# w2 at the turn between two decode layers, in six column blocks instead of four

## The chip, the cores and the metric

The kernel runs on one core of a Trainium2 chip. The metric is device time in microseconds (us) from start to end of one execution; lower is better. A time of this kernel before is the median of three executions. The core's engines are TensorE (PE, its weight loads PEld), VectorE (DVE), ScalarE (ACT), GpSimd (POOL) and SyncE (SP), which here does nothing but issue DMAs. The DMAs of SP are spread over 16 DMA engines.

## The reference

One decode step of 8 sequences goes through two identical layers (the same weights and caches serve both). A layer is attention over a cache of 4096 positions, with 32 query heads on 4 key/value heads of 128, and then a dense block with a gelu:

```
x = x + _A_ref(_layernorm(x), k_cache, v_cache, wq, wo)   # q = x @ wq; softmax(q k) v; @ wo
x = x + _B_ref(_layernorm(x), w1, b1, w2, b2)             # gelu(x @ w1 + b1) @ w2 + b2
(and both lines once more)
```

Everything is fp32. Sizes: x (8, 1, 1024); k_cache and v_cache (8, 4, 4096, 128); wq (1024, 4096); wo (4096, 1024); w1 (1024, 3584); w2 (3584, 1024).

## The kernel before

All data lies in one tile `arena` of 52 units; a unit is 1024 columns by 128 partitions (0.52 MB). `stream` is a list, written out by hand, of every DMA in its order, each with the unit at which it must land. `pump()` walks this list: it issues a DMA as soon as the units of its place are free, and stops at the first that are not. `release(slot)` frees units when the PE work that reads them has been emitted, and pumps again. So SP issues in the order of the list, and each issue waits for the last matmul that read the place.

Layer 0 reads wq, all K and V of batches 0 to 7, wo, w1 and w2; layer 1 goes through the batches from 7 down to 0, and reads K and V, wo and w1 again. wq stays in the arena from layer 0 to layer 1 (units 0 to 27 and some parked pieces), so it is read once; w2 stays from the turn to the end of layer 1.

The place of the change is the turn, the function `swap()`. There the dense block of layer 0 computes its second product, h @ w2, one column block after another, and each finished block gives two tiles of 128 rows of the new x. With each such tile kt, the query product of layer 1 can be advanced by that tile's rows of wq: `used(kt, u)` does half u (4 matmuls of 512 columns, in two accumulators) and releases the wq units, into which parts of w2 and then K tiles of layer 1 are loaded. The layernorm's mean and scale are applied afterwards (`moments`).

For a column block, `down` adds 28 row tiles (kt 0 to 27; the last four are `LAST`) in four groups of 32 partitions, DVE copies the result out (L512), two small matmuls with `bsel` sum the four groups and turn them (L516), and DVE adds them to x (L518); then come the `used` calls (L361). In the trace every fp32 matmul is two records.

In layer 1 the product with w2 is made by `down_row`, from the w2 parts that are still held; the rows `LAST` of the first 512 columns are released at the turn and read again at the end (`LATE`).

Of the kernel before, what the change touches and what calls it, by code (L numbers as in the profile page):

```python
# [10 lines left out]
ALU = mybir.AluOpType  # L11
# [3 lines left out]
P = 128  # L15
B, D = 8, 1024
# [3 lines left out]
NT = D // P  # L20
# [13 lines left out]
SCW = W // 2  # L34
N_UNIT = 52
OWN = N_UNIT - 1
UNPARK = 14
XS = B + 1
CB = D // Q4
LAST = NFT - 4  # L40
W2_PARTS = (((0, 16, 40), (16, 8, 44), (LAST, 4, 46)), ((0, 4, 47), (4, 16, 48), (20, 4, 46), (LAST, 4, 0)),
            ((LAST, 4, 1), (0, 16, 2), (16, 8, 6)), ((LAST, 4, 0), (0, 16, 8), (16, 8, 12)))
LATE_AT = 14
LATE_C = 2
LATE = ((0, 2), (2, 1), (3, 1))
# [60 lines left out]
def decode_layers(ctx: ExitStack, tc: tile.TileContext, x, kc, vc, wq, wo, w1, w2, out):  # L106
# [352 lines left out]

    w2_at = {}  # L460

    def down(y, c, kts, n0=0):

        for n, kt in enumerate(kts, n0):
            g = kt % 4
            nc.tensor.matmul(y[32 * g:32 * g + 32], h_at(kt), w2_at[c, kt], start=(n < 4), stop=(n >= NFT - 4))  # L466

    def down_row(y, kts, cs=range(CB)):

        for kt in kts:  # L470
            for c in cs:
                nc.tensor.matmul(y[32 * c:32 * c + 32], h_at(kt), w2_at[c, kt], start=(kt == 0), stop=(kt == NFT - 1))  # L472

    def w2_kts(c, i):

        k0, n, _ = W2_PARTS[c][i]
        return range(k0, k0 + n)

    def arrive(key, kts):
        slot = held[key]  # L480
        for e, kt in enumerate(kts):
            w2_at[key[1], kt] = slot.ap[:, e * Q4:(e + 1) * Q4]
        return kts

    def swap():

        ys = small_ps("s")
        nc.vector.tensor_tensor(xv, xv, b2T.unsqueeze(2).to_broadcast([P, NT, B]), ALU.add)
        pt = small_ps("pt")
        late = []  # L490
        acc = q_acc()
        stats = ()

        def used(kt, u):
            slot = held.pop(("q", kt, u))
            q_part(acc, u, kt, 0, slot.ap)
            release(slot)
            if (kt, u) == (4, 0):
                st["unparked"] = unpark()

        for c in range(CB):
            y = ys[:, c % 2 * Q4:(c % 2 + 1) * Q4]
            n = 0
            for i in range(len(W2_PARTS[c])):
                kts = arrive(("w2", c, i), w2_kts(c, i))
                down(y, c, kts, n)
                n += len(kts)
            slot = held.pop(("w2", c, [k0 for k0, _, _ in W2_PARTS[c]].index(LAST)))
            if c < LATE_C:
                release(slot)  # L510
            ysb = row_s[:, c % 2 * Q4:(c % 2 + 1) * Q4]
            nc.vector.tensor_copy(ysb, y)  # L512
            while late:
                late.pop()()
            for i in range(2):
                nc.tensor.matmul(pt[:, i * B:(i + 1) * B], ysb[:, i * P:(i + 1) * P], bsel, start=True, stop=True)  # L516
            xc = xv[:, 2 * c:2 * c + 2]
            nc.vector.tensor_tensor(xc, pt[:, 0:2 * B].rearrange("p (i b) -> p i b", b=B), xc, ALU.add)  # L518
            if c == CB - 1:
                stats = moments(pt)  # L520
            for kt in (2 * c, 2 * c + 1):
                for u in range(2):
                    if kt < NT - 1:
                        late.append(lambda kt=kt, u=u: used(kt, u))
                        if (kt, u) != (3, 1):
                            late.pop()()
                    elif u == 0:
                        spot = st.pop("unparked")
                        q_part(acc, u, kt, 0, spot.ap)
                        spot.free()  # L530
                    else:
                        slot = held.pop(("qe", 0))
                        q_part(acc, u, kt, 0, slot.ap)
                        q_part(acc, u, kt, W - KEEP, spare)
                        slot.free()
                    if c == CB - 1 and (kt, u) in ((NT - 2, 1), (NT - 1, 0)):
                        next(stats, None)
# [217 lines left out]
    def fixed(*at):  # L755
        return lambda k, i: (at[i],)

    def down_weights(key, c, kts, at):
        k0, k1 = c * NFT + kts[0], c * NFT + kts[-1] + 1
        stream.append((key, (k1 - k0) // 4, w2[0][:, k0 * Q4:k1 * Q4], (at,), ()))  # L760

    def listed(*spots):
        spots = iter(spots)
# [17 lines left out]
    for c in range(CB):  # L781
        for i, (_, _, at) in enumerate(W2_PARTS[c]):
            down_weights(("w2", c, i), c, w2_kts(c, i), at)
    stream.append((("qe", 0), 0, wq[0][:, -W:-KEEP], x_row[:, 0:W - KEEP], ()))
    batch(1, last_b, ((4, 16), (4, 20), (4, 24), (2, 14), (2, 16)), ((4, 20),))
    batch(1, last_b - 1, ((4, 24), (4, 16), (2, 14), (4, 20), (2, 36)), ((8, 28), (8, 16)))
    batch(1, last_b - 2, ((4, 36), (4, 24), (8, 28)), ((8, 16), (8, 24)))
    at = [32, 16, 24] * (4 * B)
    for b in orders[1][3:]:
# [10 lines left out]
    for layer in range(2):  # L800
        st["layer"] = layer
        b2_row = spare[:, SCW:SCW + Q4]
        hooks = {("probs", last_b): opened} if layer == 0 else {
            ("v", *v_at(last_b - 2, 0)): lambda: bias_row(b2_row, spare[:, SCW + Q4:SCW + Q4 + CH]),
            ("v", *v_at(last_b - 1, 1)): rebuild,
            ("v", *v_at(last_b - 3, 0)): bias_diag}
        last = attention(orders[layer], kept if layer == 0 else (), hooks)
        rsum = row_sums()
        project(f"o{layer}", oT, x_row, rsum, {4: last})
        rs = layernorm(x_row, rsum)  # L810
        if layer == 0:
            idle(CH)
            expand("i0", rs)
            idle(CH, Q4)
            swap()
        else:
            nc.vector.tensor_tensor(x_row, x_row, b2_row, ALU.add)
            y = []

            def turn_next():  # L820
                pending.pop(0)()

            def grow(kts, cs=range(CB)):
                if not y:
                    y.append(small_ps("s")[:, 0:Q4])
                down_row(y[0], kts, cs)

            def grown(u):
                return lambda: grow(range(GT * u, GT * (u + 1)))

            work = {u: [grown(u - 1), turn_next] for u in range(1, WIDE)}
            work[0] = [turn_next]
            work[1].append(scaled_x)
            work[WIDE] = [grown(WIDE - 1)]
            for e, kt in enumerate((3, 5)):
# [87 lines left out]
```

## Time and profile before

| | |
|---|---|
| median of 3 executions | 848.56 us (848.41 to 848.66) |
| profiled execution, its own time | 848.87 us |
| its span, first to last instruction | 847.0 us |
| busy: PE, DVE, ACT | 535.8, 192.4, 55.4 us |
| DMA | 358.51 MB, mean 423 GB/s |
| mean granted TensorE clock | 0.821 of full speed |

The span is what lies between the first and the last instruction; the execution's own time is 1.87 us longer. Busy time is a mean over stages with different limits, so it doesn't tell which engine sets the end. In the chain of waits, a row "DMA arena<-in_k_dram" starts with the issue of that DMA and lasts until its data has landed, so start plus length is the landing.

### The profile page before, as it was taken

What the parts mean: (1) busy time and instruction counts of PE and PEld (TensorE: products, weight loads), DVE (VectorE), ACT (ScalarE), POOL (GpSimd) and SP (SyncE); (2) the same over time, 40 slices, a digit from 0 to 9 for tenths busy, and PEclk for the clock granted to TensorE, in tenths of its full rate; (3) what the DMA queues carried; (4) which work ended last, traced back from release to release, by engine and by line L of the source; (5) the groups of instructions that cost most, each with busy time, mean ns of one, the idle gap of its engine ahead of it and who ended that gap; (6) DMA issues with size and microseconds to landing.
All of it is one profiled execution on the core that took longest, in us unless ns stands there. A gap on an engine that the chain in (4) does not pass through costs nothing.

```text
span 847.0 us, 9470 instructions
## 1 busy us (share of the span) xinstructions
PE 535.8 (63%) x4120; PEld 179.1 (21%) x4120; DVE 192.4 (23%) x636; ACT 55.4 (7%) x118; POOL 2.4 (0%) x14
## 2 busy tenths in 40 slices
PE   0755565656656657677778775476666576655677
PEld 0221111111111111133243222111111121212334
DVE  0013132313222231300010242232414132222011
ACT  0110000000000000000201100000000000000021
POOL 0000000000000000000000000000000000000000
PEclk9977779676876877699999897968768768788899
DMA  9999999999999999999999999999999999999997
GB/s 402 420 423 430 433 433 431 426 436 427 424 428 435 434 432 421 427 429 424 429 409 413 399 427 438 429 430 435 425 438 426 434 429 433 431 426 434 421 426 285
DMA packets 19768, 358.51 MB, mean 423 GB/s; under 512 B 2192, under 2 KB 2576, under 8 KB 4112
## 3 DMA queue, kind: packets, MB, share of 16 engines
q1 hardware_dynamic: 19584, 357.77, 99.2%
q8 instruction: 32, 0.52, 0.3%
q10 hardware_dynamic: 144, 0.15, 0.1%
q14 instruction: 8, 0.07, 0.0%
HBM read 357.78 MB, written 0.13 MB: 423 GB/s over the span
## 4 chain that ended last, share of the span: by engine, by line
DMA 73%; PE 23%; DVE 2%; issue 1%; another core or an unknown queue 1%; ACT 0%; SPq 0%; ACTq 0%; DVEq 0%
DMA arena<-in_k_dram 28%; DMA arena<-in_v_dram 21%; DMA arena<-in_w_dram 10%; DMA arena<-in_wo_dram 8%; PE sps L595 8%; PE o_ps L638 7%; DMA arena<-in_wq_dram 5%; PE y L424 2%; PE acc L361 1%; PE sps L472 1%; PE acc L306 1%; PE sps L650 1%; PE acc L303 0%; PE sps L346 0%
## 5 line engine op out<-in xcount | busy, mean ns | idle before, releaser
L595 PE MATMUL sps<-arena,qz 128*32 128x512 f32 x1024 | 162.3, 777 | 118.9 <-DMA arena<-in_k_dram 117.0
L638 PE MATMUL o_ps<-arena 128*32 128x512 f32 x512 | 87.4, 816 | 48.2 <-DMA arena<-in_v_dram 36.7
L638 PE MATMUL o_ps<-arena,spare 128*32 128x512 f32 x512 | 84.9, 782 | 40.9 <-DMA arena<-in_v_dram 34.0
L595 PEld LDWEIGHTS sps<-arena,qz 128*32 128x32 f32 x1024 | 37.7, 132 | 208.2 <-issue 169.8
L643 DVE SCALAR_TENSOR_TENSOR scr<-o_ps,bits,scr 128x128 f32<-128x128 f32 x192 | 67.3, 351 | 6.8
L641 DVE TENSOR_SCALAR scr<-o_ps,bits 128x128 f32<-128x128 f32 x64 | 22.4, 351 | 144.6 <-PE o_ps L638 144.6
L424 PE MATMUL y<-arena,oxT 128*32 128x256 f32 x512 | 37.8, 441 | 23.5 <-DMA arena<-in_wo_dram 23.5
L361 PE MATMUL acc<-arena,oxT 128*32 128x512 f32 x248 | 32.9, 671 | 6.3 <-DMA arena<-in_wq_dram 4.9
L650 PEld LDWEIGHTS sps<-bits,scr 128*128 128x128 f32 x128 | 21.7, 213 | 67.6 <-issue 48.3
L638 PEld LDWEIGHTS o_ps<-arena 128*32 128x32 f32 x512 | 16.9, 134 | 81.4 <-issue 49.1
L638 PEld LDWEIGHTS o_ps<-arena,spare 128*32 128x32 f32 x512 | 17.2, 131 | 71.7 <-issue 47.1
L600 DVE TENSOR_SCALAR_CACHE_REDUCE arena<-sps 128x512 f32<-128x512 f32 x16 | 11.1, 691 | 91.4 <-PE sps L595 91.4
L651 DVE TENSOR_TENSOR oxT<-sps,scr 128x8 f32<-128x8 f32 x64 | 10.5, 164 | 87.1 <-PE sps L650 87.1
L600 DVE TENSOR_SCALAR_CACHE_REDUCE spare<-sps 128x512 f32<-128x512 f32 x16 | 11.1, 691 | 82.4 <-PE sps L595 82.4
L619 ACT ACTIVATE sps<-arena,bits 128x512 f32<-128x512 f32 x16 | 10.9, 681 | 285.2 <-DVE scr L613 285.2
L619 ACT ACTIVATE sps<-spare,bits 128x512 f32<-128x512 f32 x16 | 10.9, 681 | 263.6 <-DVE scr L613 263.6
L650 PE MATMUL sps<-bits,scr 128*128 128x8 f32 x128 | 27.6, 288 | 0.0
L424 PEld LDWEIGHTS y<-arena,oxT 128*32 128x32 f32 x512 | 18.0, 125 | 44.0 <-DMA arena<-in_wo_dram 25.9
L303 PE MATMUL acc<-arena,oxT 128*32 128x512 f32 x160 | 20.7, 631 | 9.2 <-DMA arena<-in_w_dram 9.2
L184 PE MATMUL sps<-spare,ident 128*32 128x512 f32 (+2 forms) x60 | 24.9, 533 | 0.6 <-DVE scr L217 0.6
L609 PE MATMUL sps<-scr,bits 128*128 128x128 f32 x32 | 7.6, 322 | 22.9 <-DVE scr L605 22.9
L466 PE MATMUL sps<-arena,oxT 128*32 128x256 f32 x224 | 14.2, 382 | 5.6 <-DMA arena<-in_w_dram 5.6
(134 smaller groups left out, 248.8 us busy)
## 6 DMA issues: line engine op xcount, KB each, us to landing
arena<-in_v_dram SPq DMA_DIRECT2D x25, 4096.0 KB, 21.6
arena<-in_k_dram SPq DMA_DIRECT2D x21, 4096.0 KB, 20.6
arena<-in_k_dram SPq DMA_DIRECT2D x20, 2048.0 KB, 18.2
arena<-in_w_dram SPq DMA_DIRECT2D x16, 2048.0 KB, 12.7
arena<-in_v_dram SPq DMA_DIRECT2D x11, 2048.0 KB, 19.7
arena<-in_wo_dram SPq DMA_DIRECT2D x8, 2048.0 KB, 13.0
arena<-in_wo_dram SPq DMA_DIRECT2D x3, 4096.0 KB, 24.2
arena<-in_w_dram SPq DMA_DIRECT2D x6, 1024.0 KB, 19.6
```

The source lines that it names most:

```text
L184: nc.tensor.matmul(ps[0:32, 0:w], ident[:, 0:32], spare[:, 0:w], start=True, stop=True)
L303: nc.tensor.matmul(acc[32 * j:32 * j + 32, :], lhs, slot.ap[:, c:c + CH], start=(kt < 4), stop=(kt >= NT - 4))
L361: nc.tensor.matmul(acc[u][32 * j:32 * j + 32, d0 - j * CH:d1 - j * CH], xnT[:, kt * XS:kt * XS + 32], ap[:, d0 - c0:d1 - c0], start=(kt == ...
L424: nc.tensor.matmul(y[32 * j:32 * j + 32, 0:Q4], lhs[:, n * B:n * B + 32], slot.ap[:, c + j * Q4:c + (j + 1) * Q4], start=(n == 0), stop=(n ...
L466: nc.tensor.matmul(y[32 * g:32 * g + 32], h_at(kt), w2_at[c, kt], start=(n < 4), stop=(n >= NFT - 4))
L595: nc.tensor.matmul(ps[32 * g:32 * g + 32, :], qz[:, c:c + 32], kt[:, g * CH:(g + 1) * CH], start=(j == 0), stop=(j == HKV - 1))
L600: nc.vector.tensor_scalar(st["row", b].ap[:, half * CH:(half + 1) * CH], ps, SCALE, None, op0=ALU.mult, op1=ALU.max, accum_out=st["mx", b] ...
L619: nc.scalar.activation(pp, row[:, h * CH:(h + 1) * CH], AF.Exp, bias=bias, scale=1.0, accum_out=ls[:, h:h + 1])
L638: nc.tensor.matmul(o[32 * g:32 * g + 32, :], s[:, g], v[:, g * CH:(g + 1) * CH], start=(half == 0), stop=(half == NH - 1))
L641: nc.vector.tensor_scalar(r, o[:, 0:P], sel_t[:, 0:1], None, op0=ALU.mult)
L643: nc.vector.scalar_tensor_tensor(r, o[:, t * P:(t + 1) * P], sel_t[:, t:t + 1], r, op0=ALU.mult, op1=ALU.add)
L650: nc.tensor.matmul(po[:, 0:REP], r_s[j % 2], sel_h, start=True, stop=True)
```

## The change

w2 is cut at the turn into blocks of 128, 128, 256, 256, 128 and 128 columns (`BLOCKS`) instead of four of 256. `W2_STREAM` gives each part as first column tile, column tiles, first row tile, row tiles, unit. The last four rows of the last two blocks come in one DMA. `Q_TURN` says which halves of wq tiles are used ahead of the turning matmuls and which behind the addition of each block. The K tiles of layer 1's first two batches get other places and another order, and the unparked wq piece goes to unit 16 instead of 14.

```diff
-UNPARK = 14
+UNPARK = 16
-W2_PARTS = (((0, 16, 40), (16, 8, 44), (LAST, 4, 46)), ((0, 4, 47), (4, 16, 48), (20, 4, 46), (LAST, 4, 0)),
-            ((LAST, 4, 1), (0, 16, 2), (16, 8, 6)), ((LAST, 4, 0), (0, 16, 8), (16, 8, 12)))
+BLOCKS = ((0, 1), (1, 1), (2, 2), (4, 2), (6, 1), (7, 1))
+W2_STREAM = ((0, 1, 0, 24, 40), (0, 1, LAST, 4, 43), (1, 1, 0, 24, 44), (1, 1, LAST, 4, 47),
+             (2, 2, 0, 16, 48), (2, 2, LAST, 4, 43), (4, 2, LAST, 4, 47), (2, 2, 16, 8, 0),
+             (4, 2, 0, 16, 2), (4, 2, 16, 8, 6),
+             (6, 2, LAST, 4, 43), (6, 1, 0, 16, 8), (6, 1, 16, 8, 12), (7, 1, 0, 16, 10), (7, 1, 16, 8, 13))
+Q_TURN = (((), ((0, 0), (0, 1))), ((), ((1, 0), (1, 1))), ((), ((2, 0), (3, 0), (2, 1))),
+          (((3, 1),), ((4, 0), (4, 1), (5, 0))), (((5, 1),), ((6, 0),)), ((), ((6, 1),)))
...
-        for c in range(CB):
-            y = ys[:, c % 2 * Q4:(c % 2 + 1) * Q4]
+        for c, (k0, nk) in enumerate(BLOCKS):
+            w = nk * P
+            y = ys[:, c % 2 * Q4:c % 2 * Q4 + w]
...
-            while late:
-                late.pop()()
-            for i in range(2):
+            for kt, u in Q_TURN[c][0]:
+                used(kt, u)
+            for i in range(nk):
                 nc.tensor.matmul(pt[:, i * B:(i + 1) * B], ysb[:, i * P:(i + 1) * P], bsel, start=True, stop=True)
...
+            for kt, u in Q_TURN[c][1]:
+                used(kt, u)
+        next(stats, None)
+        spot = st.pop("unparked")
...
-    batch(1, last_b, ((4, 16), (4, 20), (4, 24), (2, 14), (2, 16)), ((4, 20),))
-    batch(1, last_b - 1, ((4, 24), (4, 16), (2, 14), (4, 20), (2, 36)), ((8, 28), (8, 16)))
+    batch(1, last_b, ((2, 14), (2, 18), (4, 20), (4, 24), (2, 16), (2, 14)), ((4, 20),))
+    batch(1, last_b - 1, ((2, 18), (4, 24), (4, 14), (4, 20), (2, 36)), ((8, 28), (8, 16)))
```

In `batch`, a pair is (units, first unit).

**On PE, from the first block of w2 to the last use of wq.** L466 is `down`, L516 the turning matmuls, L361 the query product. Before:

```order
L466 MATMUL sps<-arena,oxT 32x256 x28
L516 MATMUL sps<-bits,scr 128x8 x2
L361 MATMUL acc<-arena,oxT 32x512 x12
L466 MATMUL sps<-arena,oxT 32x256 x28
L361 MATMUL acc<-arena,oxT 32x512 x4
L516 MATMUL sps<-bits,scr 128x8 x2
L361 MATMUL acc<-arena,oxT 32x512 x16
L466 MATMUL sps<-arena,oxT 32x256 x28
L516 MATMUL sps<-bits,scr 128x8 x2
L361 MATMUL acc<-arena,oxT 32x512 x8
L564 MATMUL sps<-oxT,bits 128x8
```

The same place now, from the third block's end on (L481 is `down`, L527 the turning matmuls, L368 the query product):

```order
L368 MATMUL acc<-arena,oxT 32x512 x12
L481 MATMUL sps<-arena,oxT 32x256 x28
L368 MATMUL acc<-arena,oxT 32x512 x4
L527 MATMUL sps<-bits,scr 128x8 x2
L368 MATMUL acc<-arena,oxT 32x512 x12
L481 MATMUL sps<-arena,oxT 32x128 x28
L368 MATMUL acc<-arena,oxT 32x512 x4
L527 MATMUL sps<-bits,scr 128x8
L368 MATMUL acc<-arena,oxT 32x512 x4
L481 MATMUL sps<-arena,oxT 32x128 x28
L527 MATMUL sps<-bits,scr 128x8
L368 MATMUL acc<-arena,oxT 32x512 x4
```

Behind the last block there is now one half of a wq tile (x4) where there were two (x8), and the last two blocks have half the columns.

**On SP, from the last w2 parts to the third batch piece of layer 1.** Before:

```order
L268 DMA arena<-in_w_dram 128x4096
L268 DMA arena<-in_w_dram 128x2048
L268 DMA xb<-in_wq_dram 128x128
L268 DMA arena<-in_k_dram 128x4096 x3
L268 DMA arena<-in_k_dram 128x2048 x2
L268 DMA arena<-in_v_dram 128x4096
```

Now:

```order
L275 DMA arena<-in_w_dram 128x2048
L275 DMA arena<-in_w_dram 128x1024
L275 DMA arena<-in_w_dram 128x2048
L275 DMA arena<-in_w_dram 128x1024
L275 DMA xb<-in_wq_dram 128x128
L275 DMA arena<-in_k_dram 128x2048 x2
L275 DMA arena<-in_k_dram 128x4096 x2
L275 DMA arena<-in_k_dram 128x2048 x2
L275 DMA arena<-in_v_dram 128x4096
```

The last 6144 columns of w2 before wq's piece come in four DMAs instead of two, and the first K batch of layer 1 in six instead of five. Over the whole program SP issues 139 DMAs instead of 136, of the same bytes.

## Rows read from the trace of the kernel before

**Rows 1.** The page: busy share of the DMA engines in 40 slices.

```profile
DMA  9999999999999999999999999999999999999997
```

**Rows 2.** Windows ahead of the turn and over it: PE, PEld, DVE, ACT, POOL, PEclk, DMA, GB/s.

```profile
395.00:430.00 35.00, 26.23 (x245) 10.47 (x244) 3.47 (x15) 7.78 (x15) 0.00 (x0) 1.00 1.01 428
...
440.00:490.00 50.00, 39.99 (x396) 15.56 (x392) 9.22 (x34) 5.40 (x6) 0.20 (x1) 0.93 1.00 403
```

**Rows 3.** Chain of waits, DMAs at the turn and later: start us, us, what.

```profile
413.08 12.66 DMA arena<-in_w_dram
...
442.60 5.41 DMA arena<-in_w_dram
...
452.96 13.67 DMA arena<-in_w_dram
...
480.99 5.88 DMA arena<-in_k_dram
...
501.93 19.93 DMA arena<-in_v_dram
...
653.15 24.85 DMA arena<-in_v_dram
...
684.76 22.37 DMA arena<-in_k_dram
```

**Rows 4.** Chain of waits, work of PE and DVE at the turn.

```profile
448.06 0.68 PE sps L466 x8
...
450.12 2.83 PE acc L361 x24
...
466.68 1.11 PE sps L466 x16
...
476.79 0.70 DVE spare L542
...
479.87 1.10 PE sps L595 x8
```

**Rows 5.** Timeline of SP at the turn, single DMA issues: start us, us, what.

```profile
440.14 0.33 SPq L268 DMA_DIRECT2D arena<-in_w_dram  x1
...
463.20 0.33 SPq L268 DMA_DIRECT2D arena<-in_k_dram  x1
...
473.28 0.33 SPq L268 DMA_DIRECT2D arena<-in_k_dram  x1
...
475.54 0.33 SPq L268 DMA_DIRECT2D arena<-in_k_dram  x1
...
483.56 0.33 SPq L268 DMA_DIRECT2D arena<-in_v_dram  x1
```

**Rows 6.** DMA view, KB and us to landing: those issued at 440.14, 463.20, 475.54.

```profile
arena<-in_w_dram SPq DMA_DIRECT2D x1, 512.0 KB, 6.6
...
arena<-in_k_dram SPq DMA_DIRECT2D x1, 2048.0 KB, 13.4
...
arena<-in_k_dram SPq DMA_DIRECT2D x1, 1024.0 KB, 8.8
```

**Rows 7.** PE's groups by shape from 425 to 470 us: 256 and 128 columns.

```profile
L466 PE MATMUL sps<-arena,oxT 128*32 128x256 f32 x224 | 14.2, 382 | 5.6 <-DMA arena<-in_w_dram 5.6
...
L306 PE MATMUL acc<-arena,oxT 128*32 128x128 f32 x128 | 3.9, 274 | 2.2 <-DMA arena<-in_w_dram 2.2
```

**Rows 8.** Windows of 5 us in which the clock falls, columns as in rows 2.

```profile
465.00:470.00 5.00, 2.81 (x32) 1.55 (x28) 0.87 (x3) 0.00 (x0) 0.00 (x0) 0.83 1.02 436
470.00:475.00 5.00, 5.00 (x26) 1.10 (x18) 0.88 (x4) 0.00 (x0) 0.00 (x0) 0.50 0.99 390
```

**Rows 9.** DMA view, whole run: a DMA on an empty queue; instruction fetches.

```profile
out_dram<-xb SPq DMA_DIRECT2D x1, 128.0 KB, 1.7
...
q8 instruction: 32, 0.52, 0.3%
```

More of the change, by code (lines that the diff above doesn't have):

```diff
@@ L40 @@
 LAST = NFT - 4
-W2_PARTS = (((0, 16, 40), (16, 8, 44), (LAST, 4, 46)), ((0, 4, 47), (4, 16, 48), (20, 4, 46), (LAST, 4, 0)),
-            ((LAST, 4, 1), (0, 16, 2), (16, 8, 6)), ((LAST, 4, 0), (0, 16, 8), (16, 8, 12)))
+BLOCKS = ((0, 1), (1, 1), (2, 2), (4, 2), (6, 1), (7, 1))
[3 more added lines that the diff above has]
+             (6, 2, LAST, 4, 43), (6, 1, 0, 16, 8), (6, 1, 16, 8, 12), (7, 1, 0, 16, 10), (7, 1, 16, 8, 13))
+W2_OF = (((0, 0, 24), (0, LAST, 4)), ((1, 0, 24), (1, LAST, 4)), ((2, 0, 16), (2, LAST, 4), (2, 16, 8)),
+         ((4, LAST, 4), (4, 0, 16), (4, 16, 8)), ((6, LAST, 4), (6, 0, 16), (6, 16, 8)), ((6, LAST, 4), (7, 0, 16), (7, 16, 8)))
+Q_TURN = (((), ((0, 0), (0, 1))), ((), ((1, 0), (1, 1))), ((), ((2, 0), (3, 0), (2, 1))),
+          (((3, 1),), ((4, 0), (4, 1), (5, 0))), (((5, 1),), ((6, 0),)), ((), ((6, 1),)))
 LATE_AT = 14
@@ L460, in decode_layers, with w2_ap @@
     w2_at = {}
+    def w2_ap(k0, nk, kt):
+        at = [w2_at[k0 + i, kt] for i in range(nk)]
+        ap = at[0]
+        if nk == 2:
+            ap = bass.AP(ap.tensor, ap.offset, [ap.ap[0], (at[1].offset - ap.offset, 2), (1, P)])
+        return ap
     def down(y, c, kts, n0=0):
@@ L465, in down @@
             g = kt % 4
-            nc.tensor.matmul(y[32 * g:32 * g + 32], h_at(kt), w2_at[c, kt], start=(n < 4), stop=(n >= NFT - 4))
+            nc.tensor.matmul(y[32 * g:32 * g + 32], h_at(kt), w2_ap(*BLOCKS[c], kt), start=(n < 4), stop=(n >= NFT - 4))
     def down_row(y, kts, cs=range(CB)):
@@ L471, in down_row, with arrive @@
             for c in cs:
[L472 to L483, printed above, removed]
+                nc.tensor.matmul(y[32 * c:32 * c + 32], h_at(kt), w2_ap(2 * c, 2, kt), start=(kt == 0), stop=(kt == NFT - 1))
+    def arrive(key):
+        k0, nk, kt0, n = key[1:]
+        for e in range(n):
+            for i in range(nk):
+                at = (e * nk + i) * P
+                w2_at[k0 + i, kt0 + e] = held[key].ap[:, at:at + P]
     def swap():
@@ L489, in swap @@
         pt = small_ps("pt")
-        late = []
         acc = q_acc()
-        stats = ()
         def used(kt, u):
@@ L499, in used @@
                 st["unparked"] = unpark()
-        for c in range(CB):
-            y = ys[:, c % 2 * Q4:(c % 2 + 1) * Q4]
+        for c, (k0, nk) in enumerate(BLOCKS):
+            w = nk * P
+            y = ys[:, c % 2 * Q4:c % 2 * Q4 + w]
             n = 0
[L504 to L511, printed above, removed]
+            for of, kt0, nkt in W2_OF[c]:
+                key = next(("w2", *part[:4]) for part in W2_STREAM if (part[0], part[2]) == (of, kt0))
+                arrive(key)
+                down(y, c, range(kt0, kt0 + nkt), n)
+                n += nkt
+                if kt0 == LAST and k0 < LATE_C * 2:
+                    release(held.pop(key))
+            ysb = row_s[:, c % 2 * Q4:c % 2 * Q4 + w]
@@ L512, in swap @@
             nc.vector.tensor_copy(ysb, y)
-            while late:
-                late.pop()()
-            for i in range(2):
+            for kt, u in Q_TURN[c][0]:
+                used(kt, u)
+            for i in range(nk):
                 nc.tensor.matmul(pt[:, i * B:(i + 1) * B], ysb[:, i * P:(i + 1) * P], bsel, start=True, stop=True)
-            xc = xv[:, 2 * c:2 * c + 2]
-            nc.vector.tensor_tensor(xc, pt[:, 0:2 * B].rearrange("p (i b) -> p i b", b=B), xc, ALU.add)
-            if c == CB - 1:
+            xc = xv[:, k0:k0 + nk]
@@ L520, in swap @@
+            nc.vector.tensor_tensor(xc, pt[:, 0:nk * B].rearrange("p (i b) -> p i b", b=B), xc, ALU.add)
+            if c == len(BLOCKS) - 1:
                 stats = moments(pt)
[L521 to L537, printed above, removed]
+            for kt, u in Q_TURN[c][1]:
+                used(kt, u)
@@ L538, in swap @@
+        next(stats, None)
+        spot = st.pop("unparked")
+        q_part(acc, 0, NT - 1, 0, spot.ap)
+        spot.free()
+        next(stats, None)
+        slot = held.pop(("qe", 0))
+        q_part(acc, 1, NT - 1, 0, slot.ap)
+        q_part(acc, 1, NT - 1, W - KEEP, spare)
+        slot.free()
         arena.own_ap = spare[:, 0:SCW]
@@ L756, in fixed, with down_weights @@
         return lambda k, i: (at[i],)
-    def down_weights(key, c, kts, at):
-        k0, k1 = c * NFT + kts[0], c * NFT + kts[-1] + 1
-        stream.append((key, (k1 - k0) // 4, w2[0][:, k0 * Q4:k1 * Q4], (at,), ()))
+    def down_weights():
+        c0 = 0
+        for *part, at in W2_STREAM:
+            cols = part[1] * part[3] * P
+            stream.append((("w2", *part), -(-cols // SCW), w2[0][:, c0:c0 + cols], (at,), ()))
+            c0 += cols
     def listed(*spots):
@@ L780, in decode_layers @@
     weights(("i0",), w1[0], [4] * 7, fixed(48, 40, 44, 48, 40, 44, 48))
-    for c in range(CB):
-        for i, (_, _, at) in enumerate(W2_PARTS[c]):
-            down_weights(("w2", c, i), c, w2_kts(c, i), at)
+    down_weights()
     stream.append((("qe", 0), 0, wq[0][:, -W:-KEEP], x_row[:, 0:W - KEEP], ()))
-    batch(1, last_b, ((4, 16), (4, 20), (4, 24), (2, 14), (2, 16)), ((4, 20),))
-    batch(1, last_b - 1, ((4, 24), (4, 16), (2, 14), (4, 20), (2, 36)), ((8, 28), (8, 16)))
+    batch(1, last_b, ((2, 14), (2, 18), (4, 20), (4, 24), (2, 16), (2, 14)), ((4, 20),))
+    batch(1, last_b - 1, ((2, 18), (4, 24), (4, 14), (4, 20), (2, 36)), ((8, 28), (8, 16)))
     batch(1, last_b - 2, ((4, 36), (4, 24), (8, 28)), ((8, 16), (8, 24)))
@@ L841, in decode_layers @@
                 for i in range(n):
-                    for c in range(LATE_C):
-                        at = (i * LATE_C + c) * Q4
-                        w2_at[c, LAST + e + i] = ap[:, at:at + Q4]
+                    for k in range(2 * LATE_C):
+                        at = (i * 2 * LATE_C + k) * P
+                        w2_at[k, LAST + e + i] = ap[:, at:at + P]
                 grow(range(LAST + e, LAST + e + n))
@@ L881, in _blocks @@
     import numpy as _np
-    a = w.reshape(NFT, P, CB, Q4).transpose(1, 2, 0, 3)
-    late = a[:, 0:LATE_C, LAST:].transpose(0, 2, 1, 3)
-    return _np.concatenate([a.reshape(P, -1), late.reshape(P, -1)], 1)[None]
+    a = w.reshape(NFT, P, D).transpose(1, 0, 2)
+    parts = [a[:, t:t + n, k * P:(k + nk) * P] for k, nk, t, n, _ in W2_STREAM] + [a[:, LAST:, 0:LATE_C * Q4]]
+    return _np.concatenate([part.reshape(P, -1) for part in parts], 1)[None]
 def _start(x, b1, b2):
```

## The prediction

> **What bounds the kernel.** I began with the slices of the DMA engines: their busy share reads 9 from the first slice to the last but one [rows 1]. So the time is that of one stream of transfers, and an edit is worth what it takes out of that stream or adds to it. Then I asked where the stream runs below its pace. Ahead of the turn it moves 428 GB/s; over the 50 us of the turn 403, at a busy share of 1.00 all the same [rows 2]. Had the turn run at 428, it would have taken 50 x 403 / 428 = 47.1 us: 2.9 us is all that can be won there.
>
> Next, what part of this 2.9 us comes from SP issuing late, since that alone is what other places and another order can mend. A DMA's landing is set by the slowest of the 16 engines, so I go by landings. The price of a transfer: one of 2048 KB (2.097 MB) takes 4.90 us at 428 GB/s [rows 2]; one of 4096 KB takes 9.71, since landings at 678.00 and 707.13 stand three such DMAs apart [rows 3]. Two halves cost 2 x 4.90 - 9.71 = 0.09 us more than the whole, so that a DMA costs about 0.08 us fixed, and 1024 KB takes 2.49, 512 KB 1.28, 1536 KB 3.69, 256 KB 0.68 (estimates from these two). The chain's landings then give a balance, stretch by stretch [rows 3]:
> - 425.74 to 448.01: two DMAs of 2048 KB and one of 1024, two of 512, one of 2048, two of 512, worth 22.3 us; it took 22.27. Nothing lost.
> - 448.01 to 466.63: 512, 2048, 1024, 512, 2048 and 1024 KB, worth 17.3; it took 18.62. Lost 1.3.
> - 466.63 to 486.87: wq's 64 KB (0.2), three of 2048, two of 1024, worth 19.9; it took 20.24. Lost 0.4.
> - 486.87 to 521.86: four of 2048, two of 1024, one of 4096, worth 34.3; it took 34.99. Lost 0.7.
>
> Against this I hold the lead of an issue: how long before the landing of the previous DMA it comes. The DMA issued at 463.20 landed 13.4 us later, at 476.6, and its successor was issued at 473.28: a lead of 3.3. The next one was issued at 475.54 and landed at 484.3, and the one behind it came at 480.99: 3.3 again. That one landed at 486.87, and V's issue at 483.56 had 3.3 as well [rows 3, 5, 6]. These three leads lie on the stretch that lost 0.4. On the first stretch the DMA issued at 440.14 landed at 446.7, and its successor came at 442.60, a lead of 4.1 [rows 3, 5, 6]: that stretch lost nothing. So a lead of 4.1 is long enough for the slowest engine, and one of 3.3 costs 0.1 to 0.2. The 1.3 and the 0.7 have no short lead that I can put them to: the DMA that landed at 466.63 had been issued 13.67 earlier [rows 3]. They may be engines held up by instruction fetches, of which there are 32 in the run [rows 9]; the change doesn't take those away.
>
> **The change, part by part.**
>
> *Three more DMAs.* Two more for w2, one more for K, the bytes the same: 3 x 0.09 = 0.27 us on a queue that is never empty. The bounds: zero, if the short pieces hide behind the slower engines, and 3 x 1.7 = 5.1, if each cost what a DMA on an empty queue takes to land [rows 9]. I take 0.27: the 2048 KB DMAs of the trace stand in a full queue just as these will. Here a rule speaks against the change. The Trainium skill (DMA: Bandwidth & Descriptors, "Anatomy of one DMA — SWDGE (gpsimd) path") fits a DMA's time as about 2.0 us fixed plus its bytes, for DMAs issued by GpSimd; three more would be 6 us by it. In this trace that fixed part overlaps the transfer of the DMA ahead.
>
> *More pieces on PE and DVE.* `down` has 168 matmuls instead of 112, but the same columns: a 256-column block is 56 records at 14.2 / 224 = 0.063 us, 3.4 us; a 128-column block 56 at 3.9 / 128 = 0.030, 1.7 us [rows 7]. Four of the one cost what two of the one and four of the other cost, 13.6 us. Each block also pays the way from its last matmul over copy, turning matmuls and addition to the next: 448.74 to 450.12, 1.4 us [rows 4]. There are two more, 2.8 us of PE idle at most; the DMA queue covers them as long as the leads hold, which the next part works out. The 112 more records and their weight loads are about one more instruction fetch: zero to 1.3 us (the largest loss above), I take 0.
>
> *Other places and another order.* Here is the timetable of the changed turn. Landings follow from 425.74 and the prices: w1's last part at 430.6, then w2 at 434.3, 435.0, 438.7, 439.3, 444.2, 445.5, 446.8, 449.3, 454.2, 456.7, 457.9, 460.4, 461.7, 464.2, 465.5; K at 468.1, 470.6, 475.5, 480.4, 482.9, 485.4. PE must wait for the part at 449.3, rows 16 to 23 of the third block, and has nothing else to do then. From there, with 2.83 us for three halves of wq tiles (0.94 each) and 1.11 for eight row tiles [rows 4]:
> - third block done 450.4, turned 451.8, three halves 454.6;
> - fourth block 458.0 (its last part landed 456.7), one half 459.0, turned 459.9, three halves 462.7;
> - fifth block 464.4, one half 465.4, turned 466.2, one half 467.2;
> - sixth block 468.9, turned 470.3, one half 471.2.
>
> So from 450 on PE is never waiting for w2; it is PE that is behind, by 3.4 us when the last block is done. Cutting the last blocks in half therefore doesn't bring the end forward by what it saves behind the last landing. At 471.2 the place of the K tile at unit 24 comes free; before, that issue was at 473.28. The previous DMA lands at 475.5: lead 4.3, instead of 3.3. The rest of the query product is some 2.8 us (two halves and the moments), to 474.0, and from its end to the first score it was 476.79 to 479.87, 3.1 us [rows 4]: first scores at 477.1, the first two units read at 478.2, where the previous DMA lands at 482.9, lead 4.7; V's issue 2.6 later at 480.8, before a landing at 485.4, lead 4.6. If the 1.3 us of the second stretch is lost again, these leads are 1.3 longer. All lie above the 4.1 that cost nothing. Earlier, the shortest is that of the part at unit 47, released behind the second block at about 440.8, with the previous landing at 445.5: 4.7. So the 0.4 of the third stretch is won, and no new stall comes. Bounds: zero, if the 0.4 had another cause, to 2.9.
>
> **The sum.** -0.4 + 0.27 = -0.13 us. The profiled execution has 847.0 of span and 1.87 around it, 848.87 in all, 0.3 above the median of the runs shown; the difference goes onto the median: 848.56 - 0.13 = 848.4 us. A measurement of this kernel can tell about 0.2%, 1.7 us, from no change; this is far within.
>
> **The rivals.**
> - *The whole deficit is refilled* (faster). If most of the 16 engines, not the slowest alone, run dry at short leads, and the end goes by their mean, the turn could rise to 428 GB/s: 848.56 - 2.9 + 0.27 = 845.9. For it speaks the 403 against 428; against it, that a landing waits for the slowest engine, and only 0.4 of the losses lies by short leads.
> - *PE falls back* (slower). At the wait for the part at 449.3 PE stands idle over two us, and its clock may fall to 1.2 GHz. Before, it waited ahead of 466.68 and then had 0.83 and 0.50 granted, some 6.7 us at the low level [rows 4, 8]. Every us at that level puts PE 0.5 us back. Twice 6.7 us, in one stretch, is 6.7 us late: the lead of 4.3 becomes -2.4, and with the 1.7 us to a first landing [rows 9] the queue is empty for 4.1: 848.4 + 4.1 = 852.5. It decides the sign from about 8.6 us of low clock (4.3 late); 6.7 us, as before, leaves a lead near 1 and costs under 1 us. Against it: PE has matmuls without a gap from 451.8 on.
> - *Every DMA pays its fixed time in full* (slower): if nothing of a DMA's time from issue to landing overlapped the one ahead, 3 x 1.7 = 5.1 us by the row of the empty queue [rows 9], 853.5. Against it stands the 0.09 us between two halves and a whole. This is the mechanism behind the rule of the Trainium skill's page that I named with the three DMAs.
>
> **Chances.** The forecast, no change that shows, 0.76 (of this 0.02 each beyond the bound on either side); the deficit refilled 0.13; PE falls back 0.08; fixed times in full 0.03. Faster 0.15, within the bound 0.72, slower 0.13. The range: the forecast's own is 847.2 to 849.7 (the 0.4 with or without, one fetch of up to 1.3 more or less on the slowest engine); drawn part of the way to the cases on both sides it is 846.7 to 850.0.
>
> **What would show it.** The windows over the turn should rise from 403 GB/s to between 405 and 412. In SP's timeline, the K issue at unit 24 should come near 471 and no lead in the turn be under 4; PE should have one wait of over 2 us, for the second part of the third block, and none for w2 after it. The third stretch should cost what its prices say. I'd be wrong if the GB/s of the turn went to 425 and the end came 2 us earlier, or if leads under 2 showed with the clock at 0.50 through the 450s and 460s, or if landings in the turn stood more than 0.1 us per added DMA further apart.

## The result: slower by 0.2%, and the profile after

The changed kernel takes 850.33 us in the median of 13 executions (848.27 to 852.18), the kernel before, measured beside it, 848.56 (13 executions, 847.54 to 849.66): a ratio of 1.0021 (95% interval 1.0013 to 1.0029). The forecast of 848.4 was 1.9 us too low, and the time lies above the range. A second measurement (label e9_again, below) gave 849.70 against 848.82, 1.0015 (1.0005 to 1.0024). The profiled execution is one of the slower ones: 850.0 us of span, 851.78 in all, against 848.87 for the profiled one of before.

The windows of the changed kernel, ahead of the turn, over it, and in three pieces of 5 us (the granted clock, the DMA share and GB/s are the last three columns):

```profile
395.00:430.00 35.00, 26.39 (x245) 10.41 (x244) 3.18 (x14) 7.78 (x15) 0.00 (x0) 1.00 1.01 427
440.00:490.00 50.00, 39.63 (x479) 17.08 (x472) 8.25 (x31) 5.40 (x6) 0.20 (x1) 0.90 0.99 393
...
445.00:450.00 5.00, 2.37 (x40) 1.20 (x40) 0.00 (x0) 0.00 (x0) 0.00 (x0) 0.95 1.04 432
450.00:455.00 5.00, 4.17 (x28) 1.92 (x32) 0.60 (x2) 0.00 (x0) 0.00 (x0) 0.50 0.98 413
455.00:460.00 5.00, 5.00 (x36) 1.30 (x32) 0.00 (x0) 0.00 (x0) 0.00 (x0) 0.52 0.90 349
```

Ahead of the turn nothing differs from [rows 2]; over the turn it is 393 GB/s where before had 403 and the forecast wanted 405 to 412. The clock is down (0.50 of full speed is its level of 1.2 GHz) from the end of the first piece to the end of the third, 0.5 + 5.0 + 4.8 = 10.3 us; in before it fell later, behind 465 [rows 8].

PE's timeline in the changed kernel (L481 is `down`, L527 the turning matmuls, L368 the query product; in brackets the idle time ahead and what ended it):

```profile
445.00 2.37 PE L481 MATMUL sps<-arena,oxT 128*32 128x256 f32 x40 [0.58 <-DMA arena<-in_w_dram]
450.01 1.94 PE L481 MATMUL sps<-arena,oxT 128*32 128x256 f32 x16 [2.64 <-DMA arena<-in_w_dram]
452.49 1.02 PE L527 MATMUL sps<-bits,scr 128*128 128x8 f32 x4 [0.55 <-DVE scr L523]
453.78 5.35 PE L368 MATMUL acc<-arena,oxT 128*32 128x512 f32 x24 [0.27 <-DVE oxT L529]
...
480.57 1.92 PE L600 MATMUL sps<-arena,qz 128*32 128x512 f32 x16 [1.11 <-DVE oxT L556]
```

PE waits 2.64 us for rows 16 to 23 of the third block, as foretold. Then the same 24 records of the query product that took 2.83 in [rows 4] take 5.35, and the last eight row tiles 1.94 instead of 1.11. First scores come at 480.57, forecast 477.1, before 479.87 [rows 4].

Four of SP's issues in the changed kernel, then the DMA view of the same four (us to landing) and, of the whole run, of instruction fetches:

```profile
447.43 0.33 SPq L275 DMA_DIRECT2D arena<-in_w_dram  x1
...
455.77 0.33 SPq L275 DMA_DIRECT2D arena<-in_w_dram  x1
...
469.43 0.33 SPq L275 DMA_DIRECT2D arena<-in_k_dram  x1
...
474.72 0.33 SPq L275 DMA_DIRECT2D arena<-in_k_dram  x1
```

```profile
arena<-in_w_dram SPq DMA_DIRECT2D x1, 512.0 KB, 11.2
...
arena<-in_w_dram SPq DMA_DIRECT2D x1, 1024.0 KB, 5.3
...
arena<-in_k_dram SPq DMA_DIRECT2D x1, 2048.0 KB, 10.3
...
arena<-in_k_dram SPq DMA_DIRECT2D x1, 2048.0 KB, 10.0
...
q8 instruction: 33, 0.54, 0.3%
```

The part for units 8 and 9 is issued at 455.77, 8.3 us behind the issue ahead of it (447.43, which landed 11.2 later, at 458.6): a lead of 2.9. By the prediction's timetable its place was free at 452.7 (third block turned 451.8, one half of 0.94), 3.1 us earlier; 0.7 of that is the part that PE waited for, which let PE start at 450.01 where the prices said 449.3. The K issue at unit 24 stands at 474.72, not at 471.2. From 461.1 (455.77 + 5.3) to 484.7 (474.72 + 10.0) there land 512, 1024, 512, 64, 1024, 1024 KB and two of 2048: worth 20.0 by the prices, and it took 23.6. So 3.6 us were lost here on the slowest engine. Before had lost 1.3 + 0.4 in the prediction's second and third stretches, so that 1.9 of it came with the change, near the 1.8 between the medians. The largest piece is the K issue at 469.43: its lead is 3.3 (the DMA ahead, issued at 466.18, landed 6.6 later, at 472.8), and it lands at 479.7, 7.0 behind, for a price of 4.9.

### The profile page after: what moved, and what is told of

Read it like the earlier page. It is cut to its first block, busy times and chain, and to the rows that moved or that the text cites. A ratio compares the mean times of both kernels' runs of the same rounds, so it can differ in the third digit from the quotient of the medians.

```text
span 850.0 us, 9704 instructions
## 1 busy us (share of the span) xinstructions
PE 538.2 (63%) x4232; PEld 181.6 (21%) x4232; DVE 193.0 (23%) x640; ACT 55.6 (7%) x118; POOL 2.5 (0%) x14
## 4 chain that ended last, share of the span: by engine, by line
DMA 70%; PE 26%; DVE 2%; issue 1%; another core or an unknown queue 1%; ACT 1%; SPq 0%; ACTq 0%; DVEq 0%
DMA arena<-in_k_dram 26%; DMA arena<-in_v_dram 23%; DMA arena<-in_wo_dram 8%; PE sps L600 8%; DMA arena<-in_w_dram 8%; PE o_ps L643 8%; DMA arena<-in_wq_dram 5%; PE acc L368 2%; PE acc L310 2%; PE sps L487 1%; PE sps L481 1%; PE y L431 1%; PE sps L655 1%; PE acc L313 0%
## 5 line engine op out<-in xcount | busy, mean ns | idle before, releaser
L643 PE MATMUL o_ps<-arena,spare 128*32 128x512 f32 x512 | 81.8, 755 | 42.5 <-DMA arena<-in_v_dram 35.6
L368 PE MATMUL acc<-arena,oxT 128*32 128x512 f32 x248 | 35.4, 708 | 6.2 <-DMA arena<-in_wq_dram 4.2
L656 DVE TENSOR_TENSOR oxT<-sps,scr 128x8 f32<-128x8 f32 x64 | 10.5, 164 | 91.8 <-PE sps L655 91.8
L310 PE MATMUL acc<-arena,oxT 128*32 128x512 f32 x160 | 22.8, 690 | 8.0 <-DMA arena<-in_w_dram 7.9
L481 PE MATMUL sps<-arena,oxT 128*32 128x128 f32 (+1 forms) x336 | 14.8, 326 | 3.8 <-DMA arena<-in_w_dram 3.8
## 6 DMA issues: line engine op xcount, KB each, us to landing
arena<-in_wo_dram SPq DMA_DIRECT2D x8, 2048.0 KB, 13.5
arena<-in_wo_dram SPq DMA_DIRECT2D x3, 4096.0 KB, 23.6
```

The costliest lines, as they stand in the source:

```text
L310: nc.tensor.matmul(acc[32 * j:32 * j + 32, :], lhs, slot.ap[:, c:c + CH], start=(kt < 4), stop=(kt >= NT - 4))
L368: nc.tensor.matmul(acc[u][32 * j:32 * j + 32, d0 - j * CH:d1 - j * CH], xnT[:, kt * XS:kt * XS + 32], ap[:, d0 - c0:d1 - c0], start=(kt == ...
L481: nc.tensor.matmul(y[32 * g:32 * g + 32], h_at(kt), w2_ap(*BLOCKS[c], kt), start=(n < 4), stop=(n >= NFT - 4))
L643: nc.tensor.matmul(o[32 * g:32 * g + 32, :], s[:, g], v[:, g * CH:(g + 1) * CH], start=(half == 0), stop=(half == NH - 1))
```

## The experiments

Two theories stood against each other. **Clock theory**: the wait for the third block's last part brings PE's clock down; PE falls behind, SP issues late, the stream runs dry. **Pieces theory**: more DMAs and blocks cost by themselves. Besides, the new K places (K theory) and a late end in layer 1 (tail theory).

**Which half of the change?** e3_old_k is the changed kernel with the K places, order and `UNPARK` of before; e4_new_k is before with those of the change.

> The changed kernel with the K places and K order of before (and the unparked piece at unit 14): w2 in six blocks alone. Clock theory: the drop and its cost stay, time 850.0 to 850.6, K's issues late as with the new places. K theory (the new places and order of K cost it): time back to 848.5. Pieces theory: as the clock theory, less 0.1 for one DMA fewer.

> The kernel before with the K places and K order of the change alone (and the unparked piece at unit 16). Clock theory: no new wait ahead of 465, time 848.3 to 848.8. K theory: slower by 1 to 2 us, 849.6 to 850.6. Pieces theory: 848.7.

e3_old_k: 849.98, ratio 1.0024 (1.0014 to 1.0034). e4_new_k: 848.80, 1.0001 (0.9992 to 1.0009), with 413 GB/s over its turn. So the loss comes with the w2 blocks, and the K theory falls. How this loss came about differs: the profiled execution of e3_old_k took 851.44 with only 3.4 us of low clock and the part for units 8 and 9 issued at 454.19, which cost e5_fill5 (below) nothing. Its first K issue, with the old places, came at 463.49 with a lead of 3.6.

**A shorter wait.** e2_swap exchanges two entries of the list:

```diff
-(4, 2, LAST, 4, 47), (2, 2, 16, 8, 0),
+(2, 2, 16, 8, 0), (4, 2, LAST, 4, 47),
```

> The changed kernel with two entries of the list exchanged: the last part of the third block is issued ahead of the four last rows of the fourth. It lands 1.3 us earlier, so that PE's wait shrinks from 2.64 to 1.3 to 1.5 us. Clock theory: the clock stays at 1.00 or falls for less than the 10.3 us; leads from 455 on rise by 2 us or more; time 848.3 to 849.3. Pieces theory and tail theory: time stays at 850.0 to 850.6.

849.54 in the median, 0.2 above the expected range, ratio 1.0002 (0.9991 to 1.0012; the ratio is taken over all executions and is not that of the medians). PE's timeline, and the windows of its turn:

```profile
448.11 1.07 PE L481 MATMUL sps<-arena,oxT 128*32 128x256 f32 x16 [1.39 <-DMA arena<-in_w_dram]
```

```profile
440.00:490.00 50.00, 37.75 (x458) 16.30 (x450) 9.39 (x35) 5.40 (x6) 0.20 (x1) 0.95 1.01 415
```

The wait is half as long. The clock falls behind it all the same, for 3.4 us (0.66 from 450 to 455, 1.00 from 455 on); but the part for units 8 and 9 is issued at 452.43, and the turn moves 415 GB/s, with the same number of DMAs and blocks as the changed kernel. That speaks against the pieces theory.

**Filling the wait.** Idle matmuls of 256 columns stand ahead of that part; they write an unused piece of PSUM. The number is 18 in e1_fill, 11 in e15_fill11 and 5 in e5_fill5, all in one group of 32 partitions; e13_fill_four has 20, dealt to the four groups.

```diff
+                if (c, kt0) == (2, 16):
+                    for f in range(FILL):
+                        nc.tensor.matmul(pt[0:32, Q4:2 * Q4], ident[:, 0:32], spare[:, 0:Q4], start=True, stop=True)
```

In e13_fill_four the output is `pt[32 * (f % 4):32 * (f % 4) + 32, Q4:2 * Q4]`.

> The changed kernel with 18 idle matmuls of 256 columns (about 2.2 us, into unused columns of an accumulator) ahead of the last part of the third block, where PE waited 2.64 us and after which the clock was 0.50 from 449.5 to 459.8. Clock theory (that wait drops the clock, PE falls back some 4 us, SP issues late): clock 1.00 from 430 to 475, the w2 part that was issued at 455.77 comes near 453, no lead under 4 until 475, GB/s from 455 to 480 above 400 instead of 349 to 401, time near 848.6, ratio to before 0.999 to 1.001. Pieces theory (more DMAs and blocks cost it by themselves): clock 1.00, but the time stays at 850.0 to 850.6. Tail theory (the last 35 us of PE at a low clock cost it, and the turn doesn't matter): time stays near 850.3, with 2 us or more from the last landing to the end.

> The changed kernel with five idle matmuls of 256 columns ahead of the third block's last part (about 2.5 us at the 0.49 us that each took in the run with 18). Clock theory: the clock stays at 1.00 through the 450s, the w2 part that was issued at 455.77 comes near 453 with a lead above 5, the windows from 440 to 490 move 410 to 415 GB/s, and the time is 848.4 to 849.3, as with the exchanged list entries. Pieces theory (more blocks and DMAs cost by themselves, whatever the clock): the lead grows but the time stays at 850 or above. If the wait alone, and not the fall of the clock behind it, makes PE late, the part comes near 455 at full clock.

> The changed kernel with 20 idle matmuls of 256 columns ahead of the third block's last part, dealt to the four groups of 32 partitions in turn, so that they should take about 0.12 us each, 2.5 us together, beside the wait of 2.6 that is there anyway. If PE's clock then stays at 1.00 through the 450s and 460s, this is the turn for which the prediction worked out its timetable: the w2 part at about 452.5, the K issue at unit 24 at 471, first scores near 477, windows from 440 to 490 at 412 to 416 GB/s, and 848.4 to 848.8 (ratio 0.999 to 1.0005). If the timetable itself was wrong, the issues come 2 us later although the clock is full, and the time is 849.5 or more.

> The changed kernel with eleven idle matmuls in one group of partitions ahead of the third block's last part (5.4 us, so that PE is 2.8 us late behind the wait, between the run with five and the run with 18). Lateness theory: the w2 part comes near 455.5 with a lead near 3, as in the changed kernel with its low clock, though the clock is at 1.00 for most of the time; the windows from 440 to 490 move 400 to 405 GB/s, and the time is 849.6 to 850.4, between the 848.83 of five and the 851.66 of 18. If what costs is the low clock in some other way than by PE's lateness: 848.8 to 849.2.

e1_fill was mis-sized: its 18 took 7.9 us, and so it became the test of a PE that is late at full clock. In order of the issue for units 8 and 9 (clock and GB/s from windows and the issue from SP's timelines, each of the one profiled execution; the time lost is the ratio's, of 848.7, over all executions):

| | clock in the turn | issue | GB/s, 440 to 490 | ratio (95%) | lost, us |
|---|---|---|---|---|---|
| e13_fill_four | 1.00, 445 to 485 | 453.07 | 413 | 1.0002 (0.9993 to 1.0011) | 0.2 |
| e5_fill5 | 3.4 us low, 450 to 460 | 454.32 | 412 | 1.0000 (0.9991 to 1.0009) | 0.0 |
| e15_fill11 | 1.00, 445 to 475 | 454.96 | 409 | 1.0010 (1.0001 to 1.0019) | 0.8 |
| changed kernel | 10.3 us low, 445 to 460 | 455.77 | 393 | 1.0021 (1.0013 to 1.0029) | 1.8 |
| e1_fill | 1.00, 440 to 490 | 458.15 | 388 | 1.0039 (1.0025 to 1.0053) | 3.3 |

The leads of these issues are, in the table's order, 6.1, 4.3, 3.1, 2.9 and 0.1 us. In these five the versions with a late issue are the slow ones, whether the low clock made PE late or idle matmuls did. The first two can't be told apart, and e15_fill11 adds little: its interval begins at 1.0001, and its profiled execution took 848.94. In e5_fill5 the clock fell although its idle matmuls left a wait of only 0.49 us. Two stretches of e1_fill, windows:

```profile
450.00:455.00 5.00, 5.00 (x37) 2.62 (x36) 0.00 (x0) 0.00 (x0) 0.00 (x0) 1.00 0.97 409
455.00:460.00 5.00, 4.17 (x42) 1.69 (x41) 0.60 (x2) 0.00 (x0) 0.00 (x0) 1.00 0.48 156
```

Here PE is busy at full clock, and the DMA engines stand idle for half of the second window. e13_fill_four is the turn for which the timetable was worked out. Its PE timeline and its K issue at unit 24 with its landing:

```profile
449.45 1.07 PE L482 MATMUL sps<-arena,oxT 128*32 128x256 f32 x16 [0.47 <-DMA arena<-in_w_dram]
451.07 0.61 PE L531 MATMUL sps<-bits,scr 128*128 128x8 f32 x4 [0.55 <-DVE scr L527]
451.95 2.78 PE L369 MATMUL acc<-arena,oxT 128*32 128x512 f32 x24 [0.27 <-DVE oxT L533]
...
477.02 3.21 PE L604 MATMUL sps<-arena,qz 128*32 128x512 f32 x28 [1.10 <-DVE oxT L560]
```

```profile
471.19 0.33 SPq L276 DMA_DIRECT2D arena<-in_k_dram  x1
```

```profile
arena<-in_k_dram SPq DMA_DIRECT2D x1, 2048.0 KB, 10.5
```

Issue at 471.19 (forecast 471.2), first scores at 477.02 (477.1), and the stretch that lost 3.6 in the changed kernel runs from 461.7 (453.07 + 8.6) to 481.7 (471.19 + 10.5): 20.0 us, its price.

**PE late, with nothing changed; and DMAs alone.** e7_before_late is the kernel before with eleven idle matmuls of the first kind ahead of its fourth block's last part. e8_pieces is before with seven more w2 DMAs, for instance:

```diff
-((LAST, 4, 1), (0, 16, 2), (16, 8, 6))
+((LAST, 4, 1), (0, 8, 2), (8, 8, 4), (16, 4, 6), (20, 4, 7))
```

> The kernel before with eleven idle matmuls of 256 columns ahead of the fourth block's last part (5.4 us, of which 1.4 were waiting anyway): nothing else is changed, no part, no place, no order. Lateness theory: the K issue at 473.28 comes at about 477.3, its lead falls from 3.3 to about -0.7, the landing behind it stands 3 to 5 us further off than its price, and the time is 851 to 852.5 (ratio 1.003 to 1.005). Pieces theory: PE's lateness is covered by the queue, under 0.5 us: 848.5 to 849.1.

> The kernel before with seven more DMAs for w2 (each part of 16 row tiles in two of 8, three of 8 in two of 4), same bytes, same order on PE. By the price of 0.08 to 0.09 us for a DMA in a full queue: 0.6 us more, 848.9 to 849.4 (ratio 1.0007). Pieces theory: if the three added DMAs cost most of the 1.8 us of the change, 0.5 us each, seven cost 3.5 to 4: 852. If a smaller DMA lands its first rows earlier and PE gains by it, no change or 0.3 us less.

e7_before_late: 851.11, 1.0035 (1.0022 to 1.0048), in the expected range, though in its profile the K issue came at 474.37 with a lead of 2.4 (477.3 and -0.7 were expected), only 1.1 later than in before: the clock, which had fallen there [rows 8], stayed at 1.00. Its windows over that place:

```profile
465.00:470.00 5.00, 5.00 (x40) 2.61 (x36) 0.00 (x0) 0.00 (x0) 0.00 (x0) 1.00 0.99 417
470.00:475.00 5.00, 4.17 (x40) 1.68 (x39) 1.18 (x5) 0.00 (x0) 0.00 (x0) 1.00 0.81 344
```

PE is late, and the DMA share falls to 0.81. The landings didn't show it there: the K DMA ahead landed at 476.8 (463.25 + 13.5), this one at 481.7 (474.37 + 7.3), 4.9 apart, the price. So by the mean of the 16 engines the stream lost time where its slowest engine lost none. Two landings on, the slowest was late as well: 1024 KB issued at 481.32, with a lead of 2.8, landed 6.8 later, at 488.1, which is 4.0 behind the landing ahead (475.71 + 8.4 = 484.1) for a price of 2.5. Whether that is the same loss isn't shown.

e8_pieces: 848.91, 1.0002 (0.9994 to 1.0011), that is 0.2 us for seven DMAs, at most 0.9. For the DMAs the pieces theory falls here, and for the blocks with e13_fill_four, which has all six.

**The late end.** In the changed kernel's profile the last w2 piece landed at 844.5 and the output was issued 2.7 us behind, at 847.21; from 812.35 on the chain holds no DMA, so PE sets the end, behind a low clock in layer 1 (0.74 from 805 to 825; before 0.91). In before the last piece landed at 843.1 and the output was issued at 844.35, 1.3 us behind. So of the 2.9 us between the two profiled executions 1.4 stand at the last landing, and 1.5 come behind it. The chain of the changed kernel:

```profile
791.32 21.03 DMA arena<-in_w_dram
812.35 0.14 issue
812.48 1.89 PE acc L310 x6
...
818.20 3.54 PE acc L310 x16
```

e6_tail puts idle matmuls between the pieces of the product with wo in layer 1 and ahead of the one with w1; e10_fill_tail has these and the five at the third block; e11_swap_tail these and the exchange; e12_before_tail is before with these. e9_again is the changed kernel once more.

```diff
+            else:
+                idle_row(4 if slot.cols > W else 2)
...
+            idle_row(4)
             expand("i1", rs, work)
```

> The changed kernel with idle matmuls of 256 columns in layer 1 too: four behind each large piece of the product with wo, two behind the small one, four ahead of the product with w1 (about 2 us each time). Tail theory: the clock stays near 1.00 from 800 to 825, PE waits for DMA landings again behind 825, the end comes 1.2 to 1.6 us behind the last landing instead of 2.74, and the time falls by 0.7 to 1.4, to 849.0 to 849.6. Rival (the late end in the profile was chance, or only follows from the late stream of the turn): 850.0 to 850.6, no difference. If the idle matmuls keep the places of wo from coming free, the windows from 790 to 820 fall under 415 GB/s and it is slower than 850.6.

> The changed kernel as it is, once more: a second profile of it. Clock theory: the wait of some 2.6 us for the third block's last part is there again and the clock falls behind it; how long it stays at 0.50 (10.3 us in the first profile, 3.4 us in the run with idle matmuls in layer 1) differs from execution to execution, and with it the time; 849.5 to 851. If the fall of 10.3 us belongs to the kernel, it is there again within 1 us.

> The changed kernel with the five idle matmuls at the third block and the idle matmuls in layer 1 together. If the turn and the end each cost their part and the parts add: 848.83 less the 0.8 that layer 1's idle matmuls took off the changed kernel, 848.0 (ratio 0.999 to 1.000). If the 0.8 came from the turn of those executions and not from the end: 848.8, no difference to the five alone.

> The changed kernel with the two list entries exchanged, so that the third block's last part is the earlier DMA, and idle matmuls in layer 1. If the parts add: 849.54 - 0.8 = 848.7, perhaps 847.8 (its turn moved 415 GB/s against 403, 1.5 us of 50), so that it would be the version to beat the kernel before (ratio 0.998 to 1.000). If the end was never the limit there: 849.5.

> The kernel before with the idle matmuls in layer 1 alone. If a late end by the low clock is a chance that every version has, as the run with seven more DMAs suggests (2.5 us from last landing to end), before gains too: 848.0 to 848.5 (ratio 0.9990 to 0.9997). If only the changed kernel has a late end: 848.6 to 849.0, no change.

849.54 (1.0015, 1.0006 to 1.0023), 849.70 (1.0015), 849.28 (1.0008, 0.9999 to 1.0017), 849.14 (1.0003, 0.9994 to 1.0011) and 848.98 (1.0003, 0.9994 to 1.0012). The clock from 805 to 825 was at 1.00 in the four profiles with idle matmuls (0.83 in e9_again), but no version gained, as far as intervals of 0.8 us either way can tell: e6_tail has the ratio of e9_again, and e10_fill_tail is not below e5_fill5. So the tail theory finds no support: the late end is something that an execution can have, and it isn't seen in the medians. e9_again and e6_tail have the same turn, and their windows show how much it differs:

```profile
450.00:455.00 5.00, 3.65 (x28) 1.74 (x32) 0.60 (x2) 0.00 (x0) 0.00 (x0) 0.62 0.97 410
455.00:460.00 5.00, 5.00 (x52) 1.59 (x48) 0.00 (x0) 0.00 (x0) 0.00 (x0) 0.70 0.97 347
```

```profile
450.00:455.00 5.00, 4.18 (x32) 1.48 (x28) 0.60 (x2) 0.00 (x0) 0.00 (x0) 0.66 0.94 397
455.00:460.00 5.00, 5.00 (x77) 2.05 (x69) 0.42 (x1) 0.00 (x0) 0.00 (x0) 1.00 0.96 379
```

Behind much the same wait (2.62 and 2.68 us) the clock was low for 3.8 + 3.0 = 6.8 us in e9_again (first two rows) and for 3.4 us in e6_tail (last two). The first execution took 851.38, the second 848.94.

**Both together.** e14_swap_fill has the exchange and ten idle matmuls dealt to the four groups.

> The changed kernel with the two list entries exchanged and ten idle matmuls, dealt to the four groups, in the wait of 1.4 us that is left there. Clock theory: full clock through the turn, all leads above 6, 415 GB/s; time as with the exchange alone or up to 0.7 less, 848.6 to 849.5. If the gain of about 1 us that most of the 16 DMA engines have in the turn reached the end, it would be 847.7 and beat the kernel before; if the slowest engine sets the end, it stays within 0.5 of before.

848.95, 1.0002 (0.9994 to 1.0011), with the clock at 1.00 from 445 to 475 and the issue for units 8 and 9 at 452.51. No version here beats the kernel before, although the turns of e2_swap, e4_new_k, e5_fill5, e13_fill_four and e14_swap_fill move 412 to 415 GB/s.

## Why the prediction was wrong

- **The step that failed** is the timetable from 449.3 on: it took "2.83 us for three halves of wq tiles" and "1.11 for eight row tiles", both at full clock, right behind a wait that it had itself put at over two us. In the changed kernel they took 5.35 and 1.94. PE was 3 us late at the first issue that hung on it, the one for units 8 and 9, whose lead was 2.9 instead of the timetable's 457.9 - 452.7 = 5.2; the landings behind it lost 1.9 us more than in before, where the sum had a gain of 0.4. With the clock held up PE keeps the timetable to 0.4 us (e13_fill_four). The argument against the rival, "matmuls without a gap from 451.8 on", was no protection: the clock was down from 449.5, before these matmuls began, and stayed down through the first of them.
- **PE falls back** was the rival that happened, at a chance of 0.08: a low clock, PE late, SP late, time lost in the stream. That its formula comes near in time is luck. For 10.3 us of low clock it gives 5.2 late, a lead of -0.9 and 2.6 us of empty queue, 851.0, against 850.33 in the median and 851.78 in the profiled execution. In the trace the K issue at unit 24 was 3.5 late, and its lead was 5.0 (the landing ahead stood at 479.7). The time had been lost before it, at leads of 2.9 to 3.9, while the prediction had put a lead of 3.3 at 0.1 to 0.2 us, and leads under 2, its sign of being wrong, never showed. The rival carried the lateness to K at unit 24 alone; the first issue to come late is the w2 part for units 8 and 9, released half a wq tile behind the third block. So its limit, "from about 8.6 us of low clock", was worked out from the wrong issue; the execution of e9_again with 6.8 us took 851.38.
- **Three more DMAs** at 0.27 us: no run speaks against it; seven cost 0.2, at most 0.9 (e8_pieces). The rival of fixed times in full would have made 7 x 1.7 = 11.9 us of it and is out.
- **More pieces on PE and DVE** at nothing: right where the clock holds (e13_fill_four). One more instruction fetch came, 33 instead of the 32 of [rows 9].
- **The 0.4 of the third stretch** isn't won for certain when PE is on time. In e13_fill_four K is issued at 471.19 with a lead of 5.6, but the DMA behind it (1024 KB, lead 9.1) lands 0.4 over its price, and the bytes of the third stretch take 20.3 us, as in before (20.24); in e2_swap they take 19.9. The cause of that 0.4 stays open.

The turns with 412 to 415 GB/s bring nothing at the end, so the gain that the rival of the refilled deficit counted on doesn't get there. The traces of before and e13_fill_four show how. V's first DMA of layer 1 closes the turn with the same bytes in both. It is issued at 483.56 in before [rows 5] and lands as in the first row; the other two rows are of e13_fill_four:

```profile
arena<-in_v_dram SPq DMA_DIRECT2D x1, 2048.0 KB, 8.4
```

```profile
480.72 0.33 SPq L276 DMA_DIRECT2D arena<-in_v_dram  x1
```

```profile
arena<-in_v_dram SPq DMA_DIRECT2D x1, 2048.0 KB, 11.2
```

That is 492.0 and 491.9: the mean of the 16 engines was ahead, the slowest was not. Later the slowest is ahead for a while and loses it again. Two rows of the chain of before, and the same two landings in e13_fill_four:

```profile
626.59 22.26 DMA arena<-in_v_dram
653.15 24.85 DMA arena<-in_v_dram
```

```profile
624.55 23.21 DMA arena<-in_v_dram
652.05 25.89 DMA arena<-in_v_dram
```

The first landing comes at 648.85 and 647.76, 1.1 us earlier; the second at 678.00 and 677.94. Before needed 29.15 us between them, the price of three DMAs of 4096 KB, e13_fill_four 30.18. What held the slowest engine up there wasn't tried.

The changed list also put the wait there: a part for the fourth block stands ahead of the third block's last part. What else about a wait brings the clock down isn't settled: it fell for 3.4 us with a wait of 1.39 (e2_swap) and with one of 0.49 behind five idle matmuls in one group (e5_fill5), and stayed at 1.00 with 0.47 behind twenty in four groups (e13_fill_four).

## What to carry to other kernels

A timetable of an engine whose clock is granted must say, at each wait, at what clock the work behind it runs; price that work at both levels, and follow the lateness to the first issue that it holds up, not to the one you were looking at. Where the chunks of two consumers share a queue, put the piece that the next consumer waits for ahead of the piece for the one after. Here the slow versions were those in which PE let SP issue late, and seven more DMAs cost 0.2 us.

## What the hardware showed beyond that

- The same six blocks had the clock low for 10.3, 6.8, 3.4 and 3.4 us in four profiles (changed kernel, e9_again, e6_tail, e3_old_k), with waits of 2.6 to 2.7 us; and executions of the changed kernel spread over 3.9 us, of before over 2.1. The Trainium skill (TensorE: Matmul & The Clock Gate, "What's actually happening") says that the number of matmuls at the low clock with which a kernel starts differs from run to run of one kernel; the four profiles show as much for a fall in the middle of one.
- An idle matmul of 256 columns and 32 output partitions costs 0.44 us when all lie in one group of partitions, and 0.12 when they are dealt to four. PE's groups by shape, of e1_fill and of e13_fill_four (two records each):

```profile
L521 PE MATMUL sps<-spare,ident 128*32 128x256 f32 x36 | 7.9, 379 | 0.0
```

```profile
L521 PE MATMUL sps<-spare,ident 128*32 128x256 f32 x40 | 2.3, 379 | 0.0
```

The Trainium skill (TensorEngine Tiling (Array Packing), "Key Properties") says that different tiles of the array work in parallel; these rows agree, 7.9 / 18 = 0.44 against 2.3 / 20 = 0.12.
